# Block-causal attention and a gated FFN on one core: the last key tile of P V with all 128 rows, and two longer estimates in the kernel's own scheduler

## The chip, the cores and the metric

The kernel runs on one core of a Trainium2 chip. A core has five engines that run side by side, each through its own list of instructions in order: TensorE (PE) for matmuls, VectorE (DVE), ScalarE (ACT), GpSimd (POOL), and SyncE (SP), which here issues the DMAs. They wait for each other by semaphores. The metric is the device time of one execution in microseconds (us); the time of a kernel is the median of its runs. Beside it stands one profiled execution, whose trace gives every number on what happened when.

## The reference

q, k and v have shape (8, 8, 576, 64): 8 batches, 8 heads, 576 positions, 64 features, all in float32. The mask is causal by blocks of 64 positions: a query sees all keys of its own block and of the blocks before.

```python
scores = scale * np.matmul(q, k.transpose(0, 1, 3, 2))
mask = block_i >= block_j            # block = position // 64
scores = np.where(mask, scores, -1000000000.0)
scores = scores - np.max(scores, axis=-1, keepdims=True)
attn = np.exp(scores)
attn = attn / (np.sum(attn, axis=-1, keepdims=True) + 1e-09)
out = np.matmul(attn, v)             # then heads side by side: x, 4608 x 512
h = x @ w_in                         # 512 x 2048
g = h * np.clip(h + 3.0, 0.0, 6.0) / 6.0
return g @ w_out                     # 2048 x 512
```

## The kernel before

**Precision by halves.** Most matmuls run in float16 with each float32 operand split into a high and a low half, scaled by powers of two; three products (high x high, high x low, low x high) are added in PSUM (scores keep q's two halves on the 128 rows and take two products). The first batch's attention and the first piece of the FFN run in float32, while the weights are still being loaded and split.

**Attention.** Work goes by slots: a slot is one batch and one pair of heads, 4 slots a batch, 32 in all. Slots 0 to 3 (batch 0) use the float32 functions. For the other 28, `qk_load` brings q and k in, `qk_prep` (line 758) takes the maxima (a reduction on DVE, then a small matmul, tile mb, that spreads them over the partitions), scales and splits, and a DMA transpose on SP writes the transposed halves into tile qkT. `s_group` (line 988) handles three query blocks at a time, three groups a slot: scores on PE into PSUM tile s, the row maximum on DVE (st), exp on ACT into tile p, and high and low halves of the normalised P into tile phl (ACT and DVE). `t_dma` (line 1078) has SP transpose phl into pT: one transfer for each of the first two groups, one for each of the three query blocks of the last. `pv_group` (line 1102) then multiplies by V, twice a slot: g = 0 for query blocks 0 to 5, g = 1 for blocks 6 to 8. Both heads run in one pair of matmuls, each head on 64 of the array's 128 columns.

In `pv_group` the loop over j goes over key tiles of 128 keys. Where a range of query blocks ends on an odd block, the last key tile holds only 64 keys that count, and the kernel before uses 64 rows there:

```python
kp = BLK if 2 * j + 1 >= c1 else P
```

So it is for j = 1 of blocks 0 to 2 and for j = 4 of blocks 6 to 8: two such tiles a slot, with six matmuls each (three products, two heads). The other half of such a tile of P holds zeros: `s_group` clears the 64 columns of p behind the last key with a memset on POOL before P is split and transposed, and V's last tile has zeros behind the 576th key.

**FFN.** The tokens are cut into 13 pieces of up to 384 tokens; a piece may span the end of a batch and the start of the next. Each piece takes 16 steps, one for each 128 columns of the hidden layer: `ffn1` computes tile h (24 matmuls of 64 columns on the array), ACT and DVE make g from it, and `ffn2`, three steps behind (LAG), adds g times w_out into tile o (18 matmuls). A piece can start when every P V that writes its tokens is done. P V's results go through tile x, of which there are four buffers.

**Who sets the order.** The kernel doesn't emit its instructions directly. A `Recorder` (line 88 on) takes down every operation with what it reads and writes and a due time (`key`), then `schedule` (line 260) plays the whole program through with estimated costs, and `emit` writes the instructions in the order that came out. In the play each engine takes, of the operations that are ready and for whose tiles there is a free buffer, the one due first; an operation that may run on several engines goes to the one where it ends first. Costs are from `cost` (line 205): the time an operation keeps its engine, and the time until its result is there. For a DMA transpose the first is the time of the issue on SP (line 214), the second adds 1.1 or 2.1 us. A reader on another engine becomes ready a while after that, by a table of engines (`LAT`, line 90, in ns) at line 438:

```python
r = t if q == e and (e == "tensor" or not flow) else o.end + self.LAT[q]
```

The chip then runs the five lists as written. The estimates decide the order only; the waits on the chip are for the real results.

Of the kernel before, what the change touches and what calls it, by code (L numbers as in the profile page):

```python
# [17 lines left out]
P = 128  # L18
# [37 lines left out]
BLK = 64  # L56
# [27 lines left out]
class Recorder:  # L84
# [2 lines left out]


    NAMES = ("tensor", "vector", "scalar", "gpsimd", "sync")
    LAT = {"tensor": 55, "vector": 37, "scalar": 39, "gpsimd": 65, "sync": 65}  # L90
    TURN = 95
    BIAS = {"vector": 250.0, "gpsimd": 500.0}
    EDGE = 0.0
# [111 lines left out]
    def cost(self, eng, method, args, kw, outs, ins):  # L205


        n = self.count(outs[0])
        if method == "dma_start":
            nb = mybir.dt.size(outs[0].dtype)  # L210
            for _, c in list(outs[0].ap):
                nb *= c
            if kw.get("transpose"):
                occ = max(1290, 172 * nb / 32768 - 150)
                return occ, occ + (1100 if nb <= 4 * 32768 else 2100), False
            if eng == "gpsimd":
                return 1300, 2900 + nb / 170, False
            return 600, 2000 + nb / 170, False
        if eng == "vector":
            if method == "tensor_reduce":  # L220
                n = self.count(ins[0])
            else:
                ptr = any(isinstance(a, bass.AP) and self.count(a) == 1 for a in args[2:] if n > 1)
                ptr = ptr or n == 1 and method == "tensor_scalar_mul" and isinstance(args[2], bass.AP)
            wide = [a for a in ins if self.count(a) > 1 and not self.psum(a)]
            port = len(wide) > 1
            if method in ("tensor_scalar", "tensor_copy") and n > 1:
                if not any(self.psum(a) for a in outs + ins):
                    if len(outs[0].ap) == 2 or outs[0].ap[1][1] % 2 == 0:
                        n = n / (4 if mybir.dt.size(outs[0].dtype) + mybir.dt.size(ins[0].dtype) == 4 else 2)  # L230
                        port = True
            occ = 68 + 1.042 * n
            if method != "tensor_reduce" and ptr:
                occ += 57
            return occ, occ + 80, port
        if eng == "scalar":
            occ = 94 + 0.8335 * n
            if isinstance(kw.get("scale"), bass.AP):
                occ += 95
            if isinstance(kw.get("bias"), bass.AP):  # L240
                occ += 58
            if "accum_out" in kw:
                occ += 93
            return occ, occ + 105, False
        if eng == "gpsimd":
            if method == "memset":
                return 20 + 1.0 * n, 50 + n, False
            occ = 75 + (2.0 if method == "tensor_tensor" else 1.1) * n
            return occ, occ + 30, True
        f32 = mybir.dt.size(ins[0].dtype) == 4  # L250
        occ = max(n / 2.37, 26) * (4 if f32 else 1) + 2
        if f32 and method == "matmul":
            occ = max(occ, 200)
        if method == "transpose":
            occ = max(occ / 2, 100)
        if outs[0].ap[0][1] <= 64 and method == "matmul":
            occ = occ / 2
        return occ, occ + 172, False

    def schedule(self):  # L260
# [63 lines left out]
        while done < N:  # L324
# [110 lines left out]
            for s, flow in succ[pick]:  # L435
                rs = ready[s]
                for q in rs:
                    r = t if q == e and (e == "tensor" or not flow) else o.end + self.LAT[q]
                    rs[q] = max(rs[q], r)
# [16 lines left out]
def kernel(  # L456
# [636 lines left out]
    def place(b, t):  # L1093

        for pc, segs in enumerate(pieces):
            col = 0
            for sb, t0, t1 in segs:
                if sb == b and t0 <= t < t1:
                    return pc, col + t - t0
                col += t1 - t0  # L1100

    def pv_group(n, g):

        b, hp = divmod(n, NPAIR)
        b0, b1 = ((0, 2 * GB), (2 * GB, NB))[g]
        nt = (b1 - b0) * BLK

        parts = []
        for t0 in range(0, nt, GT):
            pc, col = place(b, b0 * BLK + t0)  # L1110
            if parts and parts[-1][0] == pc:
                parts[-1][3] += GT
            else:
                parts.append([pc, col, t0, t0 + GT])

        for pc, *_ in parts:
            while done1 < (pc - 3) * NFT or pc == 2 and done1 < NFT or pc == 3 and done2 < NFT:
                ffn_step(TOT)
            if pc in (2, 3):
                need(NCH - 1)  # L1120
        t = pT.pop((n, g))
        vv = vt[n]
        ps = ps_s.tile([P, nt], F32, tag="s", name=f"pv{n}_{g}")

        for c0, c1, u0, nu in ((b0, b1, 0, NU[2]),) if g else ((0, GB, 0, NU[0]), (GB, 2 * GB, PT_U[0], NU[1])):
            nj = (c1 + 1) // 2
            for j in range(nj):

                i0 = max(0, 2 * j - c0)
                kp = BLK if 2 * j + 1 >= c1 else P  # L1130
                a = u0 + i0 * nu + j
                us = slice(a, a + (c1 - c0 - 1 - i0) * nu + 1, nu)
                nc.joint = "pv", n, c0, j
                for si, (vl, pl) in enumerate(((0, 0), (0, 1), (1, 0))):
                    for h in range(2):
                        nc.tensor.matmul(
                            ps[h * D:(h + 1) * D, (c0 - b0 + i0) * BLK:(c1 - b0) * BLK],
                            vv[:kp, j, vl, h, :],
                            t[:kp, us, pl, h * BLK:(h + 1) * BLK],
                            start=(j == 0 and si == 0),  # L1140
                            stop=(j == nj - 1 and si == 2),
                        )
        nc.joint = None
        for pc, col, t0, t1 in parts:
            x = xb[pc % 4]
            xs = slice(col, col + t1 - t0)
            nc.scaled(x[:, 0, hp, xs], ps[:, t0:t1], E_X, "AV")
            nc.vector.scalar_tensor_tensor(
                x[:, 1, hp, xs], ps[:, t0:t1], E_X, x[:, 0, hp, xs], op0=ALU.mult, op1=ALU.subtract
            )  # L1150
# [156 lines left out]
    def ffn_step(lim):  # L1307

        nonlocal done1, done2
        if done1 < lim:  # L1310
            if done1 >= NFT:
                need(done1 % NFT // 2)
            while len(n_raw) < min(4 * (done1 // 2 + 1), 4 * NCH):
                w_ops.pop(0)()
            ffn1(*divmod(done1, NFT))
            done1 += 1
            splits()
        while done2 < done1 - LAG or (done1 == TOT and done2 < TOT):
            ffn2(*divmod(done2, NFT))
            done2 += 1  # L1320
            splits()
# [21 lines left out]
    def need(c):  # L1343

        nonlocal done2
        maxes(NCH)
        while n_split <= c:
            while done2 < 2 * n_split:
                ffn2(*divmod(done2, NFT))
                done2 += 1  # L1350
            splits(max(0, n_split + 1 - due))

    def line(points, x):

        for (x0, y0), (x1, y1) in zip(points, points[1:]):
            if x <= x1 or (x1, y1) == points[-1]:
                return y0 + (y1 - y0) * (x - x0) / (x1 - x0)
# [7 lines left out]
    for n in range(NPAIR):  # L1365
        t = AS[n]
# [8 lines left out]
    for n in range(NPAIR):  # L1375
        t = RT[n]
# [9 lines left out]
    for n in range(NPAIR, NSLOT):  # L1386
        t, d = line(AT, n), line(AT, n + 1) - line(AT, n)
        at(t - QP * d, qk_load, n, lead=QL * d)
        at(t - QP * d, qk_prep, n)
        tv = line(AT, n - NPAIR + 1)  # L1390
        if n < 2 * NPAIR:
            tv = RT[n - NPAIR] + VL1
        at(tv, v_load, n)
        b0 = n - n % NPAIR
        at(line(AT, b0 + VMX) + 0.01 * n, v_max, n)
        at(t + VP * d, v_prep, n)
        for g in range(NG):
            at(t + (g + 0.5) / NG * d, s_group, n, g)
        for g in range(2):
            at(t + (PVA, PVB)[g] * d, pv_group, n, g)  # L1400
# [30 lines left out]
    for _, _, f, a, _ in ev:  # L1431
        if f in (pv_group, pv_group32):
            for pc in fills(f, *a):
                left[pc] += 1
    for _, _, f, a, key in sorted(ev, key=lambda e: e[:2]):
        nc.key, nc.cls = key, "w" if f in (load_next, maxes, splits) else "a"
        f(*a)
        if f in (pv_group, pv_group32):
            for pc in fills(f, *a):
                left[pc] -= 1  # L1440
# [33 lines left out]
```

## Time and profile before

| | |
|---|---|
| median of 3 runs | 1071.75 us (1068.68 to 1074.57) |
| profiled execution, its own time | 1068.83 us |
| its span, first to last instruction | 1066.7 us |
| mean granted TensorE clock | 0.981 |
| busy: PE, DVE, ACT, POOL | 1005.7, 835.8, 637.0, 76.3 us |
| DMA queue of the transfers | 414064 packets, 127.05 MB, 61.3% of 16 engines |
| DMA transposes | 140 of P (phl to pT), 28 of q and k (qks to qkT) |

Nearly every operation goes through `emit`, so all of them have line 452, and the profile is read by the names of tiles: "pv<-pT,vhl" is a P V matmul that reads pT and V's halves. A form such as "128*64 128x192 f16" is 128 rows and 64 columns of the array, with 192 columns of moving data on 128 partitions. In the list of waits a row names who waited, for whom, the sum in us, how often, and the longest. A row of the timeline has the start, the length, the engine and the instruction with its count; neighbours of one name are merged under the first one's form. The ends of matmuls are modelled, so that the start of the next tile says more on the pace than the length does. Some matmul records can be missing.

### The profile page before, as it was taken

Reading aid. Unit: us, or ns where it says so; the run is one execution under the profiler, and the core shown is the slowest. Engines: PE = TensorE matmul, PEld = TensorE weight load, DVE = VectorE, ACT = ScalarE, POOL = GpSimd, SP = SyncE. Lnnn points to the kernel's source line nnn. Section 1 sums busy time; section 2 is a strip of 40 time slices with the busy share of each in tenths; the row PEclk is TensorE's granted clock in tenths of the full one; section 3 lists DMA queues with packets and bytes.
Section 4 is the critical chain, followed back from the end, with each engine's and each line's share of the span. In section 5 each row is a group of like instructions: output and inputs, shape, how many; then the busy total and the mean of one; then the engine's idle time right before and its main releaser. Section 6 shows DMA issues by size and latency. Waiting matters only on the chain. (4 is left out here: it accounts for less than half of the span.)

```text
span 1066.7 us, 28968 instructions
## 1 busy us (share of the span) xinstructions
PE 1005.7 (94%) x11588; PEld 667.8 (63%) x11588; DVE 835.8 (78%) x2308; ACT 637.0 (60%) x1548; POOL 76.3 (7%) x259
## 2 busy tenths in 40 slices
PE   6978977999999999999999999999999999999998
PEld 4646545665766776666666665766766666666664
DVE  4798999999999999999899989787898765333322
ACT  4678767656666676766677656566656553343332
POOL 3133220000000000000000000000000000000000
PEclk8898988999999999999999999999999999999999
DMA  6756547898897998888979879547656533000000
GB/s 157 185 169 175 138 109 147 132 166 149 171 159 159 153 165 141 148 166 153 156 131 179 149 121 171 110 87 131 111 98 121 97 74 57 1 31 2 31 1 31
DMA packets 414199, 128.90 MB, mean 121 GB/s; under 512 B 403184, under 2 KB 403440, under 8 KB 414064
## 3 DMA queue, kind: packets, MB, share of 16 engines
q1 hardware_dynamic: 414064, 127.05, 61.3%
q8 instruction: 91, 1.49, 0.6%
q14 instruction: 44, 0.36, 0.1%
HBM read 45.09 MB, written 9.44 MB: 51 GB/s over the span
## 5 line engine op out<-in xcount | busy, mean ns | idle before, releaser
L452 PE MATMUL h<-x,win 128*64 128x384 f16 (+2 forms) x4720 | 432.7, 321 | 1.7 <-DVE win L452 1.4
L452 PE MATMUL o<-wout,g 128*64 128x512 f16 (+3 forms) x3444 | 425.5, 379 | 2.2 <-DVE g L452 2.2
L452 PEld LDWEIGHTS <-win 128*64 128x64 f16 x4608 | 263.8, 110 | 100.9 <-issue 0.8
L452 PEld LDWEIGHTS <-g 128*64 128x64 f16 x3360 | 195.2, 110 | 130.4
L452 ACT ACTIVATE r<-h,eg,sh 128x384 f32<-128x384 f32 (+1 forms) x240 | 137.2, 593 | 132.7 <-PE h L452 130.6
L452 ACT ACTIVATE p<-s,st,esc 128x64 f32<-128x64 f32 (+1 forms) x280 | 163.0, 587 | 74.8 <-DVE st L452 54.9
L452 DVE SCALAR_TENSOR_TENSOR r<-r,eg,h 128x384 f32<-128x384 f32 (+1 forms) x192 | 113.6, 593 | 113.6 <-ACT r L452 113.5
L452 DVE SCALAR_TENSOR_TENSOR phl<-p,st,phl 128x128 f16<-128x128 f32 (+4 forms) x252 | 135.5, 583 | 1.0 <-ACT phl L452 0.9
L452 ACT ACTIVATE g<-r 128x384 f16<-128x384 f32 (+1 forms) x165 | 84.6, 514 | 82.8 <-DVE r L452 81.8
L452 DVE SCALAR_TENSOR_TENSOR g<-r,g 128x384 f16<-128x384 f32 (+1 forms) x192 | 102.9, 536 | 30.0 <-ACT g L452 29.4
L452 DVE TENSOR_REDUCE st<-s 128x1 f32<-128x64 f32 (+1 forms) x280 | 120.3, 448 | 5.0 <-PE s L452 4.6
L452 PE MATMUL s<-qkT 128*64 128x64 f16 (+7 forms) x1120 | 97.1, 289 | 7.3 <-ACT p L452 4.7
L452 PE MATMUL pv<-pT,vhl 128*64 128x192 f16 (+2 forms) x1680 | 81.1, 236 | 20.6 <-DMA pT<-phl 16.3
L452 PEld LDWEIGHTS <-vhl 128*64 128x64 f16 (+1 forms) x1680 | 69.6, 110 | 45.9 <-issue 21.8
L452 ACT ACTIVATE phl<-p,st 128x256 f16<-128x256 f32 (+4 forms) x135 | 70.6, 557 | 35.6 <-DVE st L452 17.7
L452 PEld LDWEIGHTS <-qkT 128*64 128x64 f16 x1120 | 55.3, 111 | 36.4 <-issue 10.4
L452 POOL MEMSET p<- 128x64 f32 x140 | 21.5, 154 | 528.5 <-DVE phl L452 497.1
L452 ACT ACTIVATION_READ_ACCUMULATOR p<-s,st,esc 128x1 f32 x280 | 55.1, 197 | 0.0
L452 DVE TENSOR_SCALAR phl<-p,st 128x512 f16<-128x512 f32 (+4 forms) x117 | 45.9, 423 | 1.8
L452 DVE SCALAR_TENSOR_TENSOR qks<-qk,rs_q,qks 128x576 f16<-128x576 f32 x56 | 44.7, 817 | 0.0
L452 ACT ACTIVATE x<-pv 128x192 f16<-128x192 f32 (+1 forms) x61 | 21.9, 360 | 34.4 <-PE pv L452 31.8
L452 DVE TENSOR_REDUCE qkmx<-qk 128x2 f32<-128x1152 f32 x28 | 37.7, 1346 | 0.9 <-DMA qk<-in_k_dram 0.8
(154 smaller groups left out, 825.1 us busy)
## 6 DMA issues: line engine op xcount, KB each, us to landing
out_dram<-osb SPq DMA_DIRECT2D x35, 256.0 KB, 2.4
vnat<-in_v_dram SPq DMA_DIRECT2D x64, 128.0 KB, 2.9
qk<-in_q_dram SPq DMA_DIRECT2D x28, 288.0 KB, 3.5
qk<-in_k_dram SPq DMA_DIRECT2D x28, 288.0 KB, 4.5
rawo<-in_moe_w_out_dram SPq DMA_DIRECT2D x15, 512.0 KB, 4.7
rawi<-in_moe_w_in_dram SPq DMA_DIRECT2D x14, 512.0 KB, 4.3
pT<-phl SPq DMA_TRANSPOSE x140, 3.5
vnat<-in_v_dram SPq DMA_DIRECT2D x32, 32.0 KB, 2.7
```

The source lines that it names most:

```text
L452: getattr(eng, method)(*args, **kw)
```

## The change

Three edits. P V's matmuls of the last key tile take all 128 rows of V and P instead of 64, so the multiplication includes 64 rows in which P is zero. In the scheduler's table the way from a result to TensorE grows from 55 to 855 ns. The estimate of the issue of a DMA transpose gets a third term, which is the largest from 15 blocks of 32 KB on: for q's and k's 27 blocks it gives 5400 ns instead of 4494, for the 18 blocks of P's second group 3195 instead of 2946; for the smaller ones nothing changes. Since both estimates enter the play of the whole program, the order of all five lists may come out anew.

```diff
-    LAT = {"tensor": 55, "vector": 37, "scalar": 39, "gpsimd": 65, "sync": 65}
+    LAT = {"tensor": 855, "vector": 37, "scalar": 39, "gpsimd": 65, "sync": 65}
...
-                occ = max(1290, 172 * nb / 32768 - 150)
+                occ = max(1290, 172 * nb / 32768 - 150, 245 * nb / 32768 - 1215)
...
-                kp = BLK if 2 * j + 1 >= c1 else P
...
-                            vv[:kp, j, vl, h, :],
-                            t[:kp, us, pl, h * BLK:(h + 1) * BLK],
+                            vv[:, j, vl, h, :],
+                            t[:, us, pl, h * BLK:(h + 1) * BLK],
```

## The prediction

> **What bounds the kernel now.** The page's totals come first: TensorE (PE) is busy for 94% of the span, VectorE (DVE) for 78%.
>
> ```profile
> span 1066.7 us, 28968 instructions
> ...
> PE 1005.7 (94%) x11588; PEld 667.8 (63%) x11588; DVE 835.8 (78%) x2308; ACT 637.0 (60%) x1548; POOL 76.3 (7%) x259
> ```
>
> That is an average over stages, so next comes the table of busy time in four stretches (whole program first, then the matmuls of the first FFN product, tile h, alone; those rows hold the h matmuls and the work on their results).
>
> ```profile
> 0.00:170.00 170.00, 138.94 (x786) 88.70 (x787) 138.41 (x371) 115.12 (x312) 45.79 (x98) 0.90 0.62 159
> 170.00:435.00 265.00, 253.02 (x3460) 178.14 (x3461) 254.47 (x757) 174.87 (x432) 13.54 (x67) 0.99 0.85 153
> 435.00:898.00 463.00, 448.82 (x5574) 300.87 (x5574) 393.80 (x1097) 289.18 (x699) 17.02 (x94) 1.00 0.70 127
> 898.00:1066.00 168.00, 164.91 (x1774) 100.05 (x1770) 49.17 (x85) 57.83 (x106) 0.00 (x0) 1.00 0.04 15
> ...
> 0.00:170.00 170.00, 34.16 (x176) 22.03 (x128) 5.49 (x16) 6.74 (x16) 0.90 0.62 159
> 170.00:435.00 265.00, 115.55 (x1392) 0.00 (x0) 32.35 (x59) 37.09 (x60) 0.99 0.85 153
> 435.00:898.00 463.00, 200.74 (x2196) 0.00 (x0) 56.05 (x92) 68.69 (x124) 1.00 0.70 127
> 898.00:1066.00 168.00, 85.85 (x972) 0.00 (x0) 25.18 (x41) 31.42 (x57) 1.00 0.04 15
> ```
>
> Columns are length, PE, weight loads, DVE, ACT, POOL, granted clock, DMA share, GB/s. Four regimes appear. **Start (0 to 170):** PE works 138.94 of 170 us and its granted clock is 0.90: chains of small steps, no engine full. **Early attention (170 to 435):** PE 95%, DVE 254.47 of 265, 96%: both are full. **Late attention (435 to 898):** PE 97%, DVE 85%: PE alone sets the pace. **Tail (898 on):** FFN only, PE 98%.
>
> The tile-h rows say whether PE has other work if attention is late. Two forms are the first piece's, in f32; a step of the tail shows how long one takes:
>
> ```profile
> L452 PE MATMUL h<-x,win 128*128 128x192 f32 x112 | 25.6, 355 | 1.7 <-DVE win L452 1.4 <-DVE x L452 0.3
> ...
> L452 PE MATMUL h<-x,x 128*128 128x192 f32 x16 | 3.6, 346 | 0.0
> ...
> 1049.30 1.95 PE h L452 x24
> 1051.25 1.94 PE o L452 x18
> ```
>
> The f32 piece of 16 steps takes 112 + 16 = 128 of the 176 h matmuls of the start; a later step takes 24 of h and 18 of o, 1.95 + 1.94 = 3.89 us. So (48 + 1392) / 24 = 60 of the 64 steps of pieces 1 to 4 are done at 435, where the P V that opens piece 5 stands: four steps of cover. At 898 there are 972 / 24 = 40 steps left, of which the last piece needs 16, so 24 steps of cover. So after 435 the end is PE's work plus PE's stalls; before it, a microsecond saved on PE may only become a wait for DVE. The waits of PE, start first, then 170 to 435, then 435 to 898:
>
> ```profile
> PE pt L452 <- ACT pf L452: 8.1, 5, 6.1
> PE pr L452 <- POOL rd L452: 8.0, 5, 2.9
> ...
> PE pv L452 <- DMA pT<-phl: 5.3, 5, 1.5
> PE s L452 <- ACT p L452: 4.5, 2, 3.2
> PE pv L452 <- DVE phl L452: 1.3, 1, 1.3
> PE pv L452 <- issue: 0.8, 1, 0.8
> ...
> PE pv L452 <- DMA pT<-phl: 11.0, 15, 1.1
> PE pv L452 <- ACT x L452: 0.8, 2, 0.4
> ```
>
> Nearly every stall after 170 stands ahead of a P V and is short: 5.3 + 1.3 + 0.8 = 7.4 us early, 11.0 us in 15 waits late, mean 0.73, longest 1.1.
>
> **Part 1, the last key tile with 128 rows.** Two groups of six matmuls per slot change from 64 rows to 128; columns, counts and loads stay. The forms, then two groups on PE's timeline:
>
> ```profile
> L452 PE MATMUL pv<-pT,vhl 64*64 64x64 f16 x336 | 15.7, 199 | 0.0
> ...
> 412.71 0.62 PE L452 MATMUL pv<-pT,vhl 128*64 128x192 f16 x12
> 413.27 0.52 PE L452 MATMUL h<-x,win 128*64 128x384 f16 x4
> ...
> 637.39 0.51 PE L452 MATMUL s<-qkT 128*64 128x64 f16 x12
> 637.73 2.12 PE L452 MATMUL h<-x,win 128*64 128x384 f16 x24
> ```
>
> 336 / 6 = 56 groups. The x12 of P V is six matmuls of 192 columns and six of 64, the latter on 64 rows; the x12 of scores is four each of 64, 128 and 192, all on 128 rows. Both stream 6 pairs and 768 columns a half. From start to the next tile's start P V takes 413.27 - 412.71 = 0.56 us, scores 637.73 - 637.39 = 0.34. The 0.22 us is what the group with 64 rows costs beyond its columns: the array pays to go into that shape and out again, and no other f16 form has 64 rows. 56 x 0.22 = 12.3 us. Where the matmuls fall tells how much of it counts:
>
> ```profile
> 0.00:170.00 170.00, 0.65 (x12) 0.00 (x0) 0.00 (x0) 0.90 0.62 159
> 170.00:435.00 265.00, 32.02 (x660) 11.36 (x27) 8.63 (x23) 0.99 0.85 153
> ```
>
> A group per 30 P V matmuls: 672 / 30 = 22.4 groups before 435, 33.6 after. After: 33.6 x 0.22 = 7.4 us, taken whole, since DVE has 69 us idle there. Before: 4.9 us; DVE has 10.5 us idle, so all of it or none; I take half, 2.5.
> The Trainium skill (TensorEngine Tiling (Array Packing), Performance Considerations) speaks against the edit: a contraction of 64 or less is to use row tiling, so that 64-row tiles run side by side. By it the padding would throw speed away; its rival is below. The row of 0.56 against 0.34 us does not agree.
>
> **Part 2, 800 ns more from a result to TensorE.** Nothing is added to the chip's work. In the planner every PE operation that reads another engine's or a DMA's result becomes ready 0.8 us later, so PE's list puts h and o steps ahead of it and all five lists are dealt anew: with scores move their maxima on DVE and exps on ACT, with a P V its two x operations on ACT and DVE, and on SP the transposes and the loads between them. No wait is added on the chip. A P V whose transpose lands up to 0.8 us behind plan then finds its data. With the late waits at mean 0.73 and longest 1.1, 0.8 us would cover nearly all of the 11.0. I take 60%, 6.6 us, since a new order makes some waits of its own. Early: 60% of 7.4 is 4.4; half, as above: 2.2. Bounds: all pv waits gone (18.4 us), or none net (0); below that is the rival on the other side.
> The price is latency: the broadcast of the maxima (mb), scores and P V are three PE hops a slot, 3 x 0.8 = 2.4 us. After 435 it is hidden by the 24 steps at the end, 24 x 3.89 = 93 us; four steps hide 15.6 us at 435. At 170, with 48 / 24 = 2 f16 steps done, attention has just begun and cover is thinnest: I charge 2.4 us once.
> The start: 0, with bounds of -8.0 (the pr waits behind POOL vanish) and +25.6 (last rival).
> The Trainium skill (DMA: Bandwidth & Descriptors, its fixed and variable cost components) puts a semaphore's update at about 100 ns after the receipt. By it a way of 0.1 us would be long enough, parts of 6.6 and 2.2 us would be near nothing, and the sum 16.3 - 8.8 = 7.5 us. The late waits, 0.73 us on average, point to late landings, which such a figure leaves out.
>
> **Part 3, the issue of q's and k's transposes.**
>
> ```profile
> L452 SPq DMA_TRANSPOSE qkT<-qks x28: 4026/4885/5955, 128.2 to 842.8; - x28
> DMA to landing us min/median/max: 5.9/7.6/9.1
> ...
> SPq L452 <- DVE phl L452: 200.8, 67, 8.5
> ```
>
> The formula gives 4.49 us before and 5.40 after for the 27 blocks of 32 KB (and 3.20 for 2.95 for P's second group of 18); measured 4.89. Landing was planned at 4.49 + 2.1 = 6.6, measured 7.6; now 7.5. So the plan becomes truer for landing, 0.5 us pessimistic for SP. SP itself sat 200.8 us waiting for phl, and that cover hides 28 x 0.5 = 14 us of pessimism: 0. Without it, loads of q, k, v queued behind on SP come up to 0.9 us later a slot. A gain from a truer order I count in part 2.
>
> **Sum.** 7.4 + 2.5 + 6.6 + 2.2 - 2.4 = 16.3 us. The profiled execution took 1068.83 us, 2.1 outside its span: 1052.5. It is 2.9 us under the median of the runs, near their lowest; I add half of that: 1054.
>
> **The rivals.**
> *Everything pays:* 12.3 + 18.4 = 30.7 us, 1038.1, with 1.5 added 1040. For it: early PE stalls of 7.4 us are also short. Against: DVE at 96%.
> *DVE takes it back:* before 435 nothing is gained and the P V waits only move, leaving 7.4 us: 1061.4, with 1.5 1063. For it: DVE 96%, DMA share 0.85. Against: late stalls stand where DVE idles.
> *No change:* the new order costs at unlucky places about what is saved, 16 us: 1069 to 1071. For it: all due times in the kernel stay while every ready time moves. Against: after 435 PE has always another step.
> *Row tiling after all:* the 64-row tiles overlap by themselves and padding ends that. 64 columns take 0.34 x 64 / 768 = 0.028 us a pair, three pairs 0.085; half lost is 56 x 0.042 = 2.4 us, the switch gain is gone, and 6.6 + 2.2 - 2.4 - 2.4 = 4.0 remain: 1064.8, with 1.5 1066. This is the skill's row tiling rule above.
> *Slower: the start stretches.* There the plan's extra 0.8 us becomes real, because DVE and ACT, finding the attention chain not ready in the plan, take weight work first and then run it in that order. A chain has four PE hops (q and k transposes, scores, P's transposes, P V), 3.2 us; four slots with an early and a later part make eight chains, 25.6 us. With 16.3 gained that is 9.3 us slower: 1078, with 1.5 1080. It decides once more than 16.3 + 5.4 us are lost before 170. For it: pt waits 8.1 us for exp's results, one of 6.1. Against: of those 170 us DVE is idle for 32, so weight work seldom stands in the way.
>
> **How the numbers follow.** Forecast 0.50, everything 0.17, DVE takes it back 0.13, no change 0.08, row tiling 0.04, slower 0.08. What can be told from no change is 0.5%, 5.4 us. Faster: 0.50 + 0.17 + 0.13 = 0.80; same: 0.08 + 0.04 = 0.12; slower 0.08. The range of 8 in 10 goes from 1038 to 1069: it holds the forecast (its own range 1046 to 1062), both faster rivals but for half of the lowest, row tiling and part of no change.
>
> **What would show it.** Right: no form of 64 rows among the f16 P V matmuls, P V's x12 group taking 0.34 us to the next tile's start; P V's waits for pT after 435 down from 11.0 us to under 5; attention's end, 898, earlier by about as much as the whole; DVE's busy time unchanged. Wrong: the x12 group still at 0.56; waits moved to scores or h; PE busy under 138 us of the first 170; h steps running out before 435. The forecast falls if start and early attention together are longer by more than what the late stretch saves.

## The result, and the profile after

The changed kernel takes 1044.09 us (median of 4 runs, 1042.72 to 1047.46), the kernel before 1070.22 in the runs beside it: a ratio of 0.9754, 95% interval 0.9724 to 0.9784, or 26 us less. The profiled execution of the changed kernel took 1047.46 us, the slowest of the four, so its trace shows 21 of the 26 us: spans of 1045.6 against 1066.7.

The page's totals of the changed kernel, then its busy time in the same first two stretches (columns as in the prediction; the third now ends at 875, shortly before the last P V at 878), and the h matmuls of the first two:

```profile
span 1045.6 us, 29016 instructions
...
PE 999.9 (96%) x11588; PEld 726.3 (69%) x11588; DVE 831.6 (80%) x2315; ACT 631.6 (60%) x1539; POOL 77.4 (7%) x261
```

```profile
0.00:170.00 170.00, 143.99 (x769) 89.42 (x769) 135.30 (x366) 109.05 (x303) 47.78 (x100) 0.91 0.60 155
170.00:435.00 265.00, 253.51 (x3498) 190.66 (x3498) 258.25 (x769) 181.33 (x447) 12.58 (x67) 0.99 0.89 158
435.00:875.00 440.00, 435.57 (x5522) 320.03 (x5520) 388.37 (x1096) 283.28 (x684) 17.03 (x94) 1.00 0.73 131
875.00:1045.00 170.00, 166.81 (x1810) 126.23 (x1806) 49.70 (x86) 57.94 (x107) 0.00 (x0) 1.00 0.05 18
...
0.00:170.00 170.00, 39.28 (x176) 24.90 (x128) 5.51 (x16) 6.59 (x16) 0.91 0.60 155
170.00:435.00 265.00, 117.70 (x1394) 0.00 (x0) 32.98 (x60) 37.27 (x60) 0.99 0.89 158
```

At 435 us (48 + 1394) / 24 = 60 FFN steps are done and 672 P V matmuls, both as before. So start and early attention together gained next to nothing; nearly all of the 21 us come after, 1045.6 - 435 = 610.6 us instead of 631.7. VectorE was busy for 135.30 + 258.25 = 393.6 us up to there and 392.9 before.

The P V matmuls from 435 to 898 us, from the groups of instructions (matmuls, busy time, mean in ns, idle time ahead of them and who ended it), first before, then after; then two P V groups on the timeline after:

```profile
L452 PE MATMUL pv<-pT,vhl 128*64 128x192 f16 (+2 forms) x1002 | 48.3, 235 | 13.1 <-DMA pT<-phl 11.0 <-ACT x L452 0.8 <-ACT p L452 0.6
```

```profile
L452 PE MATMUL pv<-pT,vhl 128*64 128x192 f16 (+2 forms) x1008 | 44.3, 234 | 2.3 <-ACT x L452 0.8 <-DMA pT<-phl 0.7 <-ACT qks L452 0.5
...
409.87 0.53 PE L452 MATMUL pv<-pT,vhl 128*64 128x192 f16 x12
410.21 1.30 PE L452 MATMUL h<-x,win 128*64 128x384 f16 x13
...
432.66 0.53 PE L452 MATMUL pv<-pT,vhl 128*64 128x192 f16 x12
433.00 1.71 PE L452 MATMUL o<-wout,g 128*64 128x512 f16 x14
```

The idle time ahead of P V fell from 13.1 to 2.3 us, its part from the transposes (pT) from 11.0 to 0.7. The group of twelve takes 410.21 - 409.87 = 0.34 us, what the scores' twelve took, instead of 0.56. Both named steps took place. What each is worth only the runs below can tell.

### The profile page after: what moved, and what is told of

Same layout as the page of the kernel before. It is cut to its first block, busy times and chain, and to the rows that moved or that the text cites. A ratio compares the mean times of both kernels' runs of the same rounds, so it can differ in the third digit from the quotient of the medians.

```text
span 1045.6 us, 29016 instructions
## 1 busy us (share of the span) xinstructions
PE 999.9 (96%) x11588; PEld 726.3 (69%) x11588; DVE 831.6 (80%) x2315; ACT 631.6 (60%) x1539; POOL 77.4 (7%) x261
## 5 line engine op out<-in xcount | busy, mean ns | idle before, releaser
L452 PE MATMUL h<-x,win 128*64 128x384 f16 (+2 forms) x4720 | 439.1, 323 | 11.5 <-DVE r L452 5.2
L452 PEld LDWEIGHTS <-win 128*64 128x64 f16 x4608 | 295.2, 111 | 78.5 <-issue 7.5
L452 PEld LDWEIGHTS <-g 128*64 128x64 f16 x3360 | 220.4, 110 | 105.1
L452 DVE SCALAR_TENSOR_TENSOR phl<-p,st,phl 128x256 f16<-128x256 f32 (+4 forms) x252 | 135.7, 583 | 2.1 <-ACT phl L452 1.8
L452 ACT ACTIVATE g<-r 128x384 f16<-128x384 f32 (+1 forms) x162 | 82.2, 507 | 78.9 <-DVE r L452 77.9
L452 ACT ACTIVATE phl<-p,st 128x256 f16<-128x256 f32 (+4 forms) x127 | 67.3, 564 | 34.5 <-DVE st L452 14.6
L452 PEld LDWEIGHTS <-vhl 128*64 128x64 f16 x1680 | 72.0, 110 | 19.3 <-issue 10.7
L452 PE MATMUL pv<-pT,vhl 128*64 128x192 f16 (+2 forms) x1680 | 73.6, 234 | 6.6 <-DMA pT<-phl 4.2
L452 PEld LDWEIGHTS <-qkT 128*64 128x64 f16 x1120 | 58.1, 111 | 29.9 <-issue 8.7
L452 DVE TENSOR_SCALAR phl<-p,st 128x384 f16<-128x384 f32 (+4 forms) x125 | 47.9, 414 | 1.5
```

What stands on the lines that cost most here:

```text
L452: getattr(eng, method)(*args, **kw)
```

## The experiments

Ratios are to the kernel before, run beside them on the same chip, with 95% intervals.

**One part at a time.** The rows edit doesn't enter the scheduler's costs, so it leaves the order alone: `rows_only` has the lists of before, and `lat_issue` those of the changed kernel.

`rows_only`:
```diff
-                            vv[:kp, j, vl, h, :],
-                            t[:kp, us, pl, h * BLK:(h + 1) * BLK],
+                            vv[:, j, vl, h, :],
+                            t[:, us, pl, h * BLK:(h + 1) * BLK],
```


> The kernel before with only P V's last key tile on 128 rows; all five lists stand in the order of before, word for word. Theory (late stretch pays, early stretch is shared with VectorE): 33.6 groups after 435 us times 0.22 us, 7.4 us, and of the 4.9 us before 435 little or nothing: 7 to 10 us faster, some 1061 us against 1070, with the x12 P V group at 0.34 us to the next tile's start and 60 FFN steps at 435 us as before. Rival (the price is real wherever it stands): all 56 groups pay, 12 to 13 us faster. Rival (the price belongs to matmuls of 64 columns, not of 64 rows): no change.

`lat_issue`: both estimates of the change, and `kp` as before, so 64 rows.


> The changed kernel with 64 rows put back in P V's last key tile, so both estimates are changed and nothing else; its lists stand in the order of the changed kernel. Theory: what is left of the 26 us is the waits ahead of P V (18.4 us before), so 16 to 19 us faster than before, some 1053 us, and the P V waits after 435 us near 1 us as in the changed kernel. Rival (the rows bring most of it): under 10 us faster.

`lat_only`:
```diff
-    LAT = {"tensor": 55, ...
+    LAT = {"tensor": 855, ...
```


> The kernel before with only the way to TensorE at 855 ns. Theory: the P V waits go, 14 to 19 us faster, as the two estimates together, the issue's own part being about nothing. Rival (the issue of q's and k's transposes made the plan true): under 8 us, and P V still waits over 8 us after 435 us.

`issue_only`:
```diff
-                occ = max(1290, 172 * nb / 32768 - 150)
+                occ = max(1290, 172 * nb / 32768 - 150, 245 * nb / 32768 - 1215)
```


> The kernel before with only the longer estimate of the issue of q's, k's and the middle group's transposes. Theory: within 5 us of before either way, since the landings of P's small transposes, which P V waits for, are planned as before; the late P V waits stay at 8 to 13 us. Rival: 8 us or more faster with the waits ahead of P V halved.

| kernel | median us | ratio | interval |
|---|---|---|---|
| rows_only | 1063.76 | 0.9960 | 0.9938 to 0.9982 |
| lat_issue | 1046.37 | 0.9794 | 0.9766 to 0.9822 |
| lat_only | 1059.76 | 0.9917 | 0.9887 to 0.9948 |
| issue_only | 1061.56 | 0.9938 | 0.9913 to 0.9962 |

The rows are worth 0.4%, 4.3 us (1.9 to 6.6), under the expected 7 to 10. The two estimates bring 2.1%, 22 us, so most of the change. That is more than the expected 16 to 19. Alone they bring 9 and 6.6 us, together more than their sum: the lead alone fell short of its 14 to 19 us, and that the issue's estimate would do about nothing by itself was wrong, if only just.

Where the rows' gain went is seen in P V after 435 us, with the rows alone, then with the estimates alone:

```profile
L452 PE MATMUL pv<-pT,vhl 128*64 128x192 f16 (+2 forms) x1008 | 45.1, 236 | 18.4 <-DMA pT<-phl 15.9 <-ACT p L452 0.9 <-ACT x L452 0.8
```

```profile
L452 PE MATMUL pv<-pT,vhl 128*64 128x192 f16 (+2 forms) x1008 | 47.7, 234 | 1.5 <-ACT x L452 0.8 <-ACT qks L452 0.7
```

With the rows alone, the matmuls are cheaper and the idle time ahead of them grows from 13.1 to 18.4 us. TensorE arrives earlier at the next P V and waits for the same transpose.

This can be booked from the starts of TensorE's matmuls in each trace. The mark of a float16 FFN step is the start of its last h matmul. Step 4 closes the start, step 60 stands at 435 us, step 150 at the end of attention, and between 60 and 150 the compared kernels run the same 990 P V and 640 score matmuls. There a pair of matmuls costs its columns / 2.4 + 3.3 ns when nothing is in the way (worked out from the tail: 12 pairs of 384 columns take 1.95 us, nine pairs of 512 take 1.94), 425.9 us in all; a step over 150 ns longer is booked as a stall; what is left, changes of shape and some 3 us of small float32 matmuls, is the rest.

| kernel | step 4 at, us | 4 to 60 | 60 to 150 | of it stalls | rest |
|---|---|---|---|---|---|
| before | 180.4 | 253.8 | 454.5 | 17.4 | 11.2 |
| rows_only | 177.9 | 251.4 | 455.3 | 24.8 | 4.7 |
| lat_issue | 183.2 | 247.7 | 438.7 | 2.6 | 10.2 |
| changed kernel | 184.7 | 247.8 | 436.6 | 6.8 | 4.0 |

So the changed kernel did gain 6.0 us between steps 4 and 60, as lat_issue did; its start, 4.3 us longer, ate most of it. The same booking of lat_only and issue_only tells where the surplus of the two together lies. From step 60 to 150 they just add: 9.3 and 7.1 us alone, 15.8 together. From step 4 to 60 they gain 0.4 and 2.0 alone and 6.1 together, and the start is 2.0, 4.6 and 2.8 us longer; these are single traces.

The stalls are larger here than the profile's idle times, which begin only at a matmul's modelled end; they also hold the few that don't stand ahead of P V. The rows take 6.5 us off the rest in the order of before and 6.2 in the new order, near the 33 x 0.22 = 7.3 us of the 33 groups in this stretch. But stalls grow by 7.4 and 4.2 us. Net, the stretch gets 0.8 us longer in one and 2.1 shorter in the other. The estimates take 14.8 us off the stalls.

What is gained in rows_only's trace lies ahead of step 60, 2.5 us of it ahead of step 4, where the rows play hardly a part; the orders being equal, that is one execution against another. Two traces can't place the 4.3 us of the medians.

**Which readers need the lead.** `pv_lead`: the changed kernel, where only P V gets the 855 ns.
```diff
-                    r = t if ... else o.end + self.LAT[q]
+                    r = t if ... else o.end + (self.LAT[q] if q != "tensor" or ops[s].joint and ops[s].joint[0] == "pv" else 55)
```


> The changed kernel, but only P V's matmuls get the 855 ns; every other TensorE operation has 55 ns as before. Theory (the late gain is P V's stalls): these stalls after 435 us are as in the changed kernel, near 2 us against 13.1 before, and the time is 1040 to 1050. Rival (the other hops, scores, h and o, bring the gain): P V stalls are gone but the time is above 1055.

1041.22 us, 0.9729 (0.9683 to 0.9776): as fast as the changed kernel. P V after 435 us:

```profile
L452 PE MATMUL pv<-pT,vhl 128*64 128x192 f16 (+2 forms) x1008 | 44.4, 234 | 1.4 <-ACT x L452 0.9 <-DMA pT<-phl 0.2
```

So the lead of one reader is enough here, beside the other two edits. Scores, h and o didn't need theirs.

**How much lead.** The changed kernel with 455, 955, 1655 and 2455 in place of 855, and `lat1655_64`, the one with 1655 with 64 rows.

> The changed kernel with 455 ns in place of 855, so half of the added lead. Theory: the stalls ahead of P V stand between those of before (13.1 us after 435 us) and those of the changed kernel (about 2), at 4 to 9 us, and the time is 1048 to 1058. Rival (any new order would have done, the number doesn't matter): within 3 us of 1044 or above 1060.

> The changed kernel with 955 ns instead of 855. Theory (stalls ahead of P V hardly change between the two, and the rest is the luck of the order in the start): after 435 us within 2 us of the changed kernel, the start anywhere from 126 to 140 us at the end of the first FFN piece, so a time from 1030 to 1048. Rival (the time goes smoothly with the lead): 1042, since 1655 gave 1029 and 855 gave 1044.

> The changed kernel with 1655 ns in place of 855. Theory (the P V waits that are left are late landings, and more lead hides them): P V waits after 170 us from 6.6 to under 3 us, and the time 0 to 5 us under the changed kernel's 1044. Rival (latency of the attention chain or the new order costs as much): the same or slower than 1044, up to 1055.

> The kernel with 1655 ns and the longer issue, in the same order as the run with 1655 ns, but 64 rows in P V's last key tile as before the change. The rows alone gave 4.3 us at 55 ns, where the stalls ahead of P V grew by 5.6 us after 435 us as the six matmuls got cheaper. Theory (freed time on TensorE comes back as waits for P's transposes unless there is lead): with twice the lead the rows are worth 8 to 12 us, so this kernel is 8 to 12 us slower than the one with 128 rows. Rival (the freed time is lost to another engine whatever the lead): 2 to 5 us slower.

> The changed kernel with 2455 ns instead of 855. Theory (after 435 us the stalls are gone already at 855, so more lead can pay in the start only, and costs latency where FFN steps are scarce): 1025 to 1040, and after 435 us no faster than with 1655. Rival (more lead is always better): under 1022.

| lead, ns | median us | ratio | interval | step 4 at | 4 to 60 | 60 to 150 |
|---|---|---|---|---|---|---|
| 455 | 1039.08 | 0.9737 | 0.9706 to 0.9768 | 181.4 | 245.3 | 439.8 |
| 855 | 1044.09 | 0.9754 | 0.9724 to 0.9784 | 184.7 | 247.8 | 436.6 |
| 955 | 1034.04 | 0.9655 | 0.9600 to 0.9710 | 176.8 | 243.8 | 435.4 |
| 1655 | 1028.64 | 0.9629 | 0.9609 to 0.9649 | 170.0 | 244.8 | 435.8 |
| 1655, 64 rows | 1035.04 | 0.9684 | 0.9664 to 0.9704 | 172.1 | 246.7 | 438.9 |
| 2455 | 1027.91 | 0.9598 | 0.9552 to 0.9645 | 166.6 | 248.5 | 432.4 |

From step 60 to 150 all but the last lie within 5 us (2455 ran 978 P V matmuls there, not 990, 0.4 us less of streaming, and still is 3 us shorter than 1655: against the theory more lead did pay a little there, and cost as much ahead of it). What sets the kernels apart is the start, up to 18 us, and less so steps 4 to 60, up to 5 us; and not smoothly: 955 gains 10 us on 855, and 455, expected at 1048 or more, is no slower than 855 (its trace is of its slowest run, 1045.45 us). Its idle time ahead of P V after 435 us was between those of before and of the changed kernel, as expected:

```profile
L452 PE MATMUL pv<-pT,vhl 128*64 128x192 f16 (+2 forms) x1008 | 44.7, 234 | 6.9 <-DMA pT<-phl 2.6 <-DVE rs_v L452 0.8 <-ACT x L452 0.8
```

1655 was expected to gain at most 5 us on 855, by fewer waits ahead of P V; it gained 15, nearly all of it before step 60. The rows are worth 0.55%, 6 us, at 1655: below the 8 to 12 expected with full lead. In the stretch above, some 7 us come off the rest and some 4 us return as stalls, so more lead doesn't end that.

**The start.** `start1655`: the changed kernel, with 1655 for results before 150 us of the scheduler's play.
```diff
+                    ... o.end + (1655 if q == "tensor" and o.end < 150e3 else self.LAT[q])
```


> The changed kernel, with 1655 ns instead of 855 for results that the scheduler's play places before 150 us, and 855 after. The kernel with 1655 throughout finished its first FFN piece at 126 us of the trace against 137 in the changed kernel, and was 15 us faster. Theory (that gain is the start's new order, and the later lead adds little): the first piece ends near 126 us and the time is 1029 to 1035. Rival (the larger lead is needed throughout): 1038 or more.

1030.73 us, 0.9630 (0.9584 to 0.9676), as with 1655 throughout. The start of this kernel, all engines, then h:

```profile
0.00:170.00 170.00, 144.25 (x870) 93.99 (x872) 148.32 (x405) 120.11 (x324) 45.92 (x104) 0.94 0.64 166
...
0.00:170.00 170.00, 40.39 (x222) 23.01 (x128) 7.22 (x19) 8.56 (x19) 0.94 0.64 166
170.00:435.00 265.00, 120.45 (x1430) 0.00 (x0) 32.91 (x60) 37.50 (x60) 0.99 0.92 158
```

(222 - 128) / 24, almost 4 float16 steps, are done at 170 us instead of 2, and 63.5 at 435 instead of 60: step 4 is passed at 170.1 us, 14.6 earlier, against 13.4 us gained in the medians. VectorE does 148.3 us of work in those first 170 instead of 135.3, TensorE about the same. That the new order of the start brings the gain is shown. That it is the length of the lead, and not the luck of an order, isn't: step 4 stands at 181.4, 184.7 and 176.8 us with 455, 855 and 955 ns. How the order does it stays open too. That it keeps VectorE at work is one reading of these rows, but a start that gets further has more of every engine's work in it. TensorE's clock is a rival: granted 0.90 in the first 170 us before and 0.91 in the changed kernel, it is 0.94 here, and 0.92, 0.94, 0.94 and 0.96 with 455, 955, 1655 and 2455 ns. An estimate from these: 0.03 of 170 us is 5 us at full clock, a third of the gain. No run tells whether the clock is a cause of the shorter start or comes with it.

**The price of 64 rows by itself.** `ffn64`: the changed kernel, one of four row tiles of each float16 h step on 64 rows. The sums leave out the other 64 rows.
```diff
-                        win[:, f * P // NH, d, wl, fc + h * BLK:fc + (h + 1) * BLK],
-                        x[:, xl, d, :w],
+                        win[:BLK if d == 1 else P, f * P // NH, d, wl, fc + h * BLK:fc + (h + 1) * BLK],
+                        x[:BLK if d == 1 else P, xl, d, :w],
```


> The changed kernel, in its own order, with the second of the four row tiles of each float16 step of the first FFN product on 64 rows; the sums leave out the other 64 rows of that tile. Six matmuls in each of 192 steps, so 192 goes into the shape and out of it. Theory (the price is 0.22 to 0.24 us for each, by rows and not by columns, and TensorE is the bound): 42 to 46 us slower than the changed kernel, of which 41 steps x 0.23 = 9.4 us in the tail. Rival (the price belongs to matmuls of 64 columns): no slower. Rival (half of it hides in waits): 20 to 30 us.

1073.4 us, 29 us above the changed kernel. The chain of waits in the tail (start, length, work), in the changed kernel and in ffn64:

```profile
1000.96 1.95 PE h L452 x24
1002.90 1.94 PE o L452 x18
```

```profile
1002.79 2.19 PE h L452 x24
1004.98 1.94 PE o L452 x18
```

The same 24 matmuls of 384 columns cost 0.24 us more, by rows and not by columns, and the rival of 64 columns falls. 192 x 0.24 = 46 us of work was added and 29 us of time: the rival in which part hides holds. In the tail nothing hides: its last 42 steps take 10.0 us longer, and 42 x 0.24 is 10.1. In steps 60 to 150 the rest grows by 19.6 us (90 x 0.24 = 21.6) and the stalls fall from 6.8 to 1.2, so 14.0 us are paid. It is the rows edit run backwards.

## Why the prediction was right, and where it was not

The time, 1044.1, lies in the range 1038 to 1069, and faster was the likely sign. The forecast of 1054 was 10 us too slow, and its sum had the wrong weights: too much for the rows, too little for the estimates. That these two errors partly cancel is luck. The rival in which everything pays, 1040, came nearer, but not by its terms either, as it counted 12.3 us for the rows.

- **What bounds the kernel.** Early attention was said to be shared with VectorE, and the saving there was counted at half, 2.5 + 2.2 us. Steps 4 to 60 gained 6.0, all of it from the estimates (lat_issue 6.1; the rows on top nothing, though rows_only's trace has 2.4 there), so the sum was near and its parts were not. For late attention "PE alone sets the pace" was the step that failed. TensorE's pace there is its work plus its stalls, and the stalls answer to its work: less work, more stall (rows_only, 7.4 us), more work, less stall (ffn64, 5.6 us). Only in the tail is a microsecond a microsecond. The rivals that VectorE takes the early gain back, and that nothing changes, fell.
- **Part 1.** The price of 0.22 us and its cause were right (0.34 us after; 0.24 us in ffn64's tail). The term 7.4 + 2.5 = 9.9 us measured 4.3 (1.9 to 6.6) in the old order and 6 at 1655 ns. The row tiling rival fell: the group takes 0.34 us with 128 rows and 0.56 with 64, and the rows alone made the kernel faster, not slower.
- **Part 2.** The mechanism was right, and pv_lead puts it at P V alone. The size was wrong twice. I took 60% of the late waits, and 13.1 - 2.3 = 10.8 of 13.1 us of idle time went; and the idle times understate a stall, as the booking of all stalls shows: 17.4 - 2.6 = 14.8 us. 6.6 + 2.2 us measured 22 together with part 3 (20 in the trace). The 2.4 us charged for latency can't be told apart: at 855 ns the start is 2.8 and 4.3 us longer in the two traces of this order, but at 955 and more, where that price would be higher, it is shorter. The rival in which a way of 0.1 us is long enough fell: with 455 ns 6.9 us of idle time are left ahead of P V after 435 us, 2.6 of them for pT, with 855 ns 2.3 and 0.7. That fits late landings, the prediction's reading; the landings weren't compared with the plan's. The figure weighed there, a semaphore's update of about 100 ns, stands in the Trainium skill (DMA: Bandwidth & Descriptors, its fixed and variable cost components) for DMAs issued by GpSimd, while SP issues them here.
- **Part 3.** Counted at 0; alone it gave 6.6 us (4.1 to 9.3). Without it the lead gives 9 us, with it 22. Why the two together are worth more than their sum stays open. After 435 us each alone leaves idle time ahead of P V (4.7 us with the lead, 10.0 with the issue, 1.5 with both), but there their gains add; the surplus lies ahead of step 60, and a new order is part of each.
- **The start.** 0, with bounds of -8.0 and +25.6; the trace has +4.3 us at step 4. The pr waits fell (8.0 to 2.9 us) and h waits came, a move that the prediction named as a sign of being wrong, as these rows of the changed kernel show, the first two from its first 170 us, the last from 170 to 435:

```profile
PE h L452 <- DVE g L452: 4.9, 3, 2.7
...
PE pr L452 <- POOL rd L452: 2.9, 2, 2.5
...
PE h L452 <- DVE r L452: 5.2, 1, 5.2
```

The last one ends at 177 us, before step 4.

The rival of a stretched start had the place right and the size far too large: at 855 ns a sixth of its 25.6 us, and at 955 and more the start got shorter.

Of the signs of being right: the form with 64 rows is gone, the x12 group is at 0.34, the late waits for pT are under 5 us, attention ended earlier, 878 for 898 us by the last P V, and VectorE's busy time is near the same, 831.6 for 835.8 us.

## What to carry to other kernels

Where an in-order engine meets late data at many points, cheaper work on it can come back as waiting: here, after step 60, all of some 6 us in the order of before, and more than half with lead. Count a cut in full only where no wait follows. In a planner, an estimate that leaves room for late data can be worth more than a tight one, and one reader may be all that needs it. An order that is dealt anew can move another stage by nearly as much as the effect under study (the start by up to 18 us, beside 26 for the whole change), so test the estimate at several values: 1655 and 2455 ns gave 1028.6 and 1027.9 us, faster than both kernels.

## What the runs showed of the hardware

A change between 128 and 64 rows costs 0.22 to 0.24 us there and back, with 64 or 384 columns alike. And where P V makes no such change, the weight loads of the array's two column halves overlap less: of the w_in loads before and after, same number and mean length, the time in which at least one runs rises by 31 us.

```profile
L452 PEld LDWEIGHTS <-win 128*64 128x64 f16 x4608 | 263.8, 110 | 100.9 <-issue 0.8
```

```profile
L452 PEld LDWEIGHTS <-win 128*64 128x64 f16 x4608 | 295.2, 111 | 78.5 <-issue 7.5
```

It is the same with the rows alone (295.6 us), and with the estimates alone it is 256.7, so the rows do it, not the order. It lasts beyond attention: from 900 to 1000 us, where neither kernel has a matmul on 64 rows, the w_in loads keep 43.5 us busy (617 loads) instead of 35.1 (621). No loss of pace shows: in the tail 24 h matmuls take 1.95 us in both kernels. Why it happens wasn't tried.
